# RMS norm of two units at once with its reciprocal root on 128x8, its steps and the weight splits spread over each group, weight sums on VectorE

## The chip, the cores and the metric

The kernel runs on one core of one Trainium2 chip. The core has TensorE (matrix products into PSUM), VectorE, ScalarE and GpSimd (elementwise work; VectorE and ScalarE also read PSUM, GpSimd here works on SBUF alone) and SyncE, called SP in the profile, whose queue issues nearly all DMAs. Each engine runs its own instructions strictly in order and waits on semaphores for the others. The metric is the device time of one execution in microseconds, the median of several runs.

## What is computed

Three stages in a chain: a linear attention with decay over 768 steps for 4 batches and 8 heads, a first expert with a maximum of three products, and a second, gated expert behind an RMS norm. The norm and the second expert are where most of the change lies.

```python
# attention: y = r (state + u k v), state = w state + k v, along 768 steps; x = its output, 3072 tokens x 384
# first expert (d_ff 768)
h = np.maximum(np.maximum(x @ w1, x @ w2), x @ w3)
x = h @ w_out
# second expert (d_ff 1536)
rms = np.sqrt(np.mean(x * x, axis=-1, keepdims=True) + 1e-06)
xn = x / rms * rms_g
g = xn @ w_gate
silu = g * (1.0 / (1.0 + np.exp(-g)))
val = xn @ w_val
out = silu * val @ w_out
```

## The kernel before

**Units and pairs.** Tokens are cut into units of 512 columns; the first 512 are two half units for the first expert. Feature dimensions lie on the partitions, tokens on the free axis. The first expert runs through units 0 to 6 (`UNITS`, the last one is `L` = 6), each with 18 slots `a_l1(u, f, w)` (one 128-row block of one of the three products, nine matmuls) and, from unit 1 on, 6 slots `a_out` (nine matmuls each). Between the slots of one unit the attention steps of the next units are put, and until they are used up also the conversion of the weights (`tick`): loads as 64-bit words, an exponent cast on ScalarE, three bit operations on VectorE, and then a split or, for the second expert's weights, a store to `w2d` and the sums of `w_sums` (four subtractions of 128x128 per block f, stored to `w2t`).

**fp32 by three products.** Each fp32 operand is a high part (a cast to fp32r) and a low part (value minus high part). `mm3` (L72 to L74) issues three matmuls for a product. The cast is always on ScalarE, the subtraction on VectorE or GpSimd.

**Second expert.** It runs over three pairs of 512-token units, p = 0, 1, 2, each in 12 groups f (128 hidden features). Each group forms 2x2 blocks with fewer products: `form_steps` makes three sets of combined activations (one, y, two), `w_sums` made the combined weights. In a group, TensorE runs product A into bank a, ScalarE copies it to bank b (`pb`, L753), TensorE runs E (into `px`, L72 to L74 with `px<-f`) and adds to bank b, ScalarE copies E to `es` (L757) and bank b to c (`pc`), TensorE goes on with a, c, b, ScalarE computes `si`, copies c to d (`pd`), VectorE forms `v` and `si` (L773, L776), ScalarE casts `hb` (L704), VectorE subtracts (L705), and forms the second unit's `v` and `h` (L782, L783). `es` and both `v` share three buffers. The `b_out` products of the group before stand in the same group: block d = 0 after E, d = 1 and 2 at the end. After group 11 the even unit's three blocks are copied out (`ob`, L717), and then the odd unit's 12 `b_out` follow from `h2`, with the forms of the next pair beside them.

**Norm.** `rms_steps(u)` (L536 to L579) is a generator for one unit: squares on ScalarE, two additions on GpSimd, split, two matmuls against ones (every partition then holds the sum), and on 128x512: mean on VectorE, square root on ScalarE, four reciprocals of 128x128, a correction of five operations, three scalings. For units 0 and 1 it is drawn two steps a slot beside the first expert's last unit (from slot 2), then `form_steps(0)`. For the later pairs it is drawn four steps at the end of each group from group 2 on.

**Splits of the second expert's weights.** `ws_split` and `wo_split` make high and low parts of block f. For blocks 0 to 2 it is done in the last unit (GpSimd subtracts), for later ones in pair 0, at the end of each group, behind the norm's steps, on ScalarE and VectorE. `ws_raw` and `wo_raw` load the raw blocks; the split blocks are stored to `w2s` through GpSimd's queue and loaded from there in pairs 1 and 2 (`ws_load`).

The order on each engine is the order in which the program is written.

## Time and profile before

| | us |
|---|---|
| median of 3 runs | 949.53 (947.66 to 950.11) |
| the profiled execution, its own time | 948.55 |
| its span, first to last instruction | 946.8 |
| TensorE busy | 875.8 (92%) |
| VectorE busy | 591.3 (62%) |
| ScalarE busy | 394.5 (42%) |
| GpSimd busy | 242.5 (26%) |
| mean granted TensorE clock | 0.969 of full speed |

The rows further down are of that one execution, and times in them are microseconds from the start of the span. The first expert's last unit starts at 418.36 us and the second expert at about 477 us. A granted clock of 1.00 is 2.4 GHz, 0.50 is 1.2 GHz. In a row of the timeline the bracket at the end tells how long the engine stood idle before the instruction and what released it.

### The profile page before, as it was taken

The numbers are of one execution on the slowest core, as the hardware profiler recorded it, in microseconds if no ns is written. First come the engines' busy times: TensorE is split into PE (matmuls) and PEld (weight loads), VectorE is DVE, ScalarE is ACT, GpSimd is POOL, SyncE is SP. The second block draws the span as 40 slices with busy tenths as digits, with TensorE's granted clock in tenths as the row PEclk, the third lists the DMA queues.
The fourth block names the chain that finished last, engine by engine and source line by source line (L and its number), as shares of the span: only waits on it lengthen the run. The fifth ranks groups of instructions, "written<-read, shape, count | busy, mean of one in ns | idle before, by whom it ended". The sixth has DMA issues, their size and how long they took to land.

```text
span 946.8 us, 11983 instructions
## 1 busy us (share of the span) xinstructions
PE 875.8 (92%) x4340; PEld 731.9 (77%) x4340; DVE 591.3 (62%) x876; ACT 394.5 (42%) x744; POOL 242.5 (26%) x239
## 2 busy tenths in 40 slices
PE   7779799999989989999889887999998999999997
PEld 7678788888878878887667665878787778888875
DVE  6999738787787877736665665672453574433342
ACT  3545333323323423313365644553454444444442
POOL 2675643553554543303421000000101000000000
PEclk8789999999999999999889989999999999999999
DMA  6655434455555555443246451153422033433001
GB/s 211 209 159 165 146 117 114 138 167 176 138 175 164 155 174 160 154 160 144 101 167 216 169 194 56 50 233 145 154 102 100 1 109 157 142 109 137 14 34 37
DMA packets 48994, 128.99 MB, mean 136 GB/s; under 512 B 6176, under 2 KB 22560, under 8 KB 44320
## 3 DMA queue, kind: packets, MB, share of 16 engines
q1 hardware_dynamic: 47200, 113.99, 37.1%
q0 software_dynamic: 1728, 14.16, 3.9%
q8 instruction: 36, 0.59, 0.3%
q14 instruction: 30, 0.25, 0.1%
HBM read 92.34 MB, written 33.82 MB: 133 GB/s over the span
## 4 chain that ended last, share of the span: by engine, by line
PE 62%; DVE 19%; ACT 6%; issue 6%; DMA 2%; POOL 2%; SPq 1%; DVEq 0%; POOLq 0%; ACTq 0%
PE px L73 5%; PE px L74 5%; PE px L72 5%; PE pl L72 4%; PE pl L73 4%; PE pl L74 4%; PE pa L74 3%; PE pa L72 3%; PE pa L73 3%; PE pb L72 3%; PE pb L74 3%; PE pb L73 3%; PE py L349 2%; PE pc L72 2%; PE pc L73 2%
## 5 line engine op out<-in xcount | busy, mean ns | idle before, releaser
L72 PE MATMUL pl<-x,w_a 128*128 128x512 f32 (+1 forms) x378 | 144.1, 381 | 9.9 <-DVE c L429 6.4
L73 PE MATMUL pl<-x,w_a 128*128 128x512 f32 (+1 forms) x378 | 138.7, 367 | 0.3 <-DVE x L365 0.3
L74 PE MATMUL pl<-x,w_a 128*128 128x512 f32 (+1 forms) x378 | 138.2, 366 | 0.3 <-POOL w_a L127 0.3
L773 DVE TENSOR_TENSOR v<-pb,es 128x512 f32<-128x512 f32 x36 | 24.9, 691 | 151.9 <-PE pb L74 143.1
L72 PEld LDWEIGHTS pl<-x,w_a 128*128 128x128 f32 x378 | 73.7, 195 | 20.9 <-DVE c L429 5.7
L72 PE MATMUL px<-hb,wo 128*128 128x512 f32 x216 | 84.5, 391 | 3.6 <-ACT hb L704 3.6
L73 PE MATMUL px<-hb,wo 128*128 128x512 f32 x216 | 84.5, 391 | 0.7 <-DVE hb L705 0.7
L74 PE MATMUL px<-hb,wo 128*128 128x512 f32 x216 | 84.2, 390 | 0.0
L74 PEld LDWEIGHTS pl<-x,w_a 128*128 128x128 f32 x378 | 73.5, 194 | 11.5 <-POOL w_a L127 0.5
L73 PEld LDWEIGHTS pl<-x,w_a 128*128 128x128 f32 x378 | 73.7, 195 | 9.7 <-DVE x L365 0.6
L431 ACT CAST h1h<-c 128x512 fp32r<-128x512 f32 (+1 forms) x42 | 23.5, 559 | 119.3 <-DVE c L429 119.3
L349 PE MATMUL py<-Dg,tm 128*96 128x128 f32 x368 | 57.9, 284 | 10.8 <-DVE Dg L302 9.8
L429 DVE TENSOR_TENSOR c<-pl,c 128x512 f32<-128x512 f32 (+1 forms) x84 | 50.6, 602 | 26.7 <-PE pl L74 19.1
L257 ACT ACTIVATE rh<-raw,csb 96x512 fp32r<-96x512 f32 (+1 forms) x48 | 32.1, 715 | 70.1 <-DVE raw L247 55.2
L72 PE MATMUL pb<-f,ws 128*128 128x512 f32 x108 | 44.6, 413 | 15.5 <-ACT pb L753 15.5
L704 ACT CAST hb<-si 128x512 fp32r<-128x512 f32 x36 | 22.3, 621 | 85.7 <-DVE si L776 85.7
L302 DVE COPY_PREDICATED Dg<-csb,pa 128x512 f32<-128x512 uint32 x48 | 35.0, 730 | 36.6 <-PE pa L74 17.7
L349 PEld LDWEIGHTS py<-Dg,tm 128*96 128x96 f32 x368 | 47.0, 170 | 13.5 <-DVE Dg L302 11.8
L118 DVE SCALAR_TENSOR_TENSOR wf<-wraw,wf 128x384 uint32<-128x384 uint32 x60 | 55.5, 924 | 0.0
L72 PEld LDWEIGHTS px<-hb,wo 128*128 128x128 f32 x216 | 40.6, 188 | 13.1 <-ACT hb L704 4.8
L113 DVE SCALAR_TENSOR_TENSOR wf<-wraw,wf 128x384 uint32<-128x384 uint32 x60 | 49.7, 828 | 0.0
L73 PEld LDWEIGHTS px<-hb,wo 128*128 128x128 f32 x216 | 40.6, 188 | 10.0 <-DVE hb L705 1.6
(172 smaller groups left out, 2143.9 us busy)
## 6 DMA issues: line engine op xcount, KB each, us to landing
ws<-w2s SPq DMA_DIRECT2D x24, 1152.0 KB, 5.2
wraw<-in_w2p SPq DMA_DIRECT2D x36, 384.0 KB, 3.6
w2s<-ws POOLq DMA_DIRECT2D x12, 1152.0 KB, 5.8
raw<-in_rkT SPq DMA_DIRECT2D x24, 384.0 KB, 4.3
tm<-in_rkv SPq DMA_DIRECT2D x24, 384.0 KB, 3.9
tm<-in_rkv SPq DMA_DIRECT2D x24, 288.0 KB, 3.1
wraw<-in_w1p SPq DMA_DIRECT2D x18, 384.0 KB, 3.6
w2d<-wf SPq DMA_DIRECT2D x36, 192.0 KB, 3.8
```

Source lines behind the costliest of these rows:

```text
L72: pe.matmul(o, lh, rh, start=start, stop=False, **kw)
L73: pe.matmul(o, lh, rl, start=False, stop=False, **kw)
L74: pe.matmul(o, ll, rh, start=False, stop=stop, **kw)
L113: dve.scalar_tensor_tensor(out=wu, in0=conv_words(n)[0], scalar=29, in1=wu, op0=ALU.logical_shift_right, op1=ALU.bitwise_or)
L118: dve.scalar_tensor_tensor(out=wu, in0=conv_words(n)[1], scalar=0x80000000, in1=wu, op0=ALU.bitwise_and, op1=ALU.bitwise_or)
L257: act.activation(rh[:, :, j], raw[:, 0], AF.Copy, scale=m01[0:96, j:j + 1])
L302: dve.copy_predicated(out=dg, mask=cmask.unsqueeze(1).to_broadcast([128, 4, 128]), data=pa.rearrange("p q j t -> p (q j) t"))
L349: pe.matmul(py[0:96, pr], tm[:, VO + 144 * pr + 48 * j:VO + 144 * pr + 48 * j + 96], s["Dg"][:, 2 * pr + j], start=(c == 0 and j == 0), st ...
L429: dve.tensor_tensor(out=c1[:, :n], in0=p[:, :n], in1=c1[:, :n], op=ALU.max)
L431: act.copy(hh, c1[:, :n])
L704: act.copy(hh, x)
L773: dve.tensor_tensor(out=v1, in0=Bk, in1=es, op=ALU.add)
```

## The change

- `norm_steps(p)` takes the place of `rms_steps(u)`: it does both units of a pair. The sums still come from two matmuls against ones, but only row 0 is copied out (1x512) and stored to a small DRAM tensor `msd`; it is loaded back as 128x8 for both units, the reciprocal root is made there by a bit estimate and four Newton steps on VectorE (16 operations, no square root on ScalarE), stored to `rsd`, and loaded back spread over all partitions; then the six scalings. `sq` has two buffers for it.
- In the pairs, one step of the norm and one of the splits is drawn at each of four places of a group (`back(0)` to `back(3)`), in place of all at the end; the splits' subtractions in pair 0 go to GpSimd.
- In the last unit of the first expert the norm is drawn from slot 1 on; its activations `h1` lie in what becomes `h2`, and the pool of the second expert is opened ahead of slot 0. The forms of pair 0 come in the order one, two, y, with the last set after slot 18.
- `w_sums` runs on VectorE and one tick later, when the third block of f is stored.
- The output blocks are tiles of their own, 128x512, in two buffers, and each is stored by itself.

```diff
     def w_sums(f, g, v):
         def sub(o, a, b):
-            pool.tensor_tensor(out=o, in0=a, in1=b, op=ALU.subtract)
+            dve.tensor_tensor(out=o, in0=a, in1=b, op=ALU.subtract)
...
-            if q == 0:
-                conv_put.g = w
-            elif q == 1:
-                w_sums(f, conv_put.g, w)
+            if q < 2:
+                conv_put.gv.append(w)
+            else:
+                w_sums(f, *conv_put.gv)
+                conv_put.gv = []
...
+        def norm_steps(p):
+            br = sB["r"]
+            us = (2 * p, 2 * p + 1)
+            x = [x2s.pop(u) for u in us]
+            sq = [br.tile([128, 3, 512], F32, tag="sq", bufs=2, name=f"sq{u}") for u in us]
+            for j in range(2):
+                for k in range(3):
+                    act.activation(sq[j][:, k], x[j][:, k], AF.Square)
+                    if k:
+                        pool.tensor_tensor(out=sq[j][:, 0], in0=sq[j][:, 0], in1=sq[j][:, k], op=ALU.add)
+                    yield
+            for j in range(2):
+                sr = br.tile([128, 2, 512], F32R, tag="sr", name=f"sr{us[j]}")
+                act.copy(sr[:, 0], sq[j][:, 0])
+                yield
+                dve.tensor_tensor(out=sr[:, 1], in0=sq[j][:, 0], in1=r32(sr[:, 0]), op=ALU.subtract)
+                yield
+                ps = psx.tile([128, 512], F32, tag="x", name=f"ss{us[j]}") if p == 0 else PX[3]
+                pe.matmul(ps, ones, sr[:, 0], start=True, stop=False)
+                pe.matmul(ps, ones, sr[:, 1], start=False, stop=True)
+                act.copy(sq[j][0:1, 1], ps[0:1])
+                sync.dma_start(msd[p, j:j + 1], sq[j][0:1, 1])
+                yield
+            m, y, t = (br.tile([128, 8], F32, tag=f"n{n}", name=f"n{n}{p}") for n in range(3))
+            sync.dma_start(m, msd[p].rearrange("j (a b) -> (j a) b", b=8))
+            yield
+            yield
...
+            for _ in range(4):
+                dve.tensor_tensor(out=t, in0=y, in1=m, op=ALU.mult)
+                dve.tensor_tensor(out=t, in0=t, in1=y, op=ALU.mult)
+                dve.scalar_tensor_tensor(out=y, in0=t, scalar=1.5, in1=y, op0=ALU.add, op1=ALU.mult)
+            sync.dma_start(rsd[p].rearrange("j (a b) -> (j a) b", b=8), y)
+            for j in range(2):
+                sync.dma_start(sq[j][:, 2], rsd[p, j].partition_broadcast(128))
             yield
             yield
+            for j in range(2):
+                for k in range(3):
+                    dve.scalar_tensor_tensor(out=x[j][:, k], in0=x[j][:, k], scalar=rg_sb[:, k:k + 1],
+                                             in1=sq[j][:, 2], op0=ALU.mult, op1=ALU.mult)
                     yield
+                xr[us[j]] = x[j]
...
-                    if n >= 2:
-                        next(es, None)
-                        next(es, None)
+                    if n >= 1:
+                        for _ in range(2):
+                            if n >= 18 or form_left[0] > 3:
+                                next(es, None)
...
-                    if d == 0:
-                        b_out.ob = br.tile([128, 3, 512], F32, tag="ob", name=f"ob{u}")
-                    ob = b_out.ob
-                    (dve.tensor_copy if d == 1 else act.copy)(ob[:, d], po[d])
-                    if u == NB - 1:
-                        sync.dma_start(out[u, :, d], ob[:, d])
-                    elif d == 2:
-                        sync.dma_start(out[u], ob)
+                    ob = br.tile([128, 512], F32, tag="ob", bufs=2, name=f"ob{u}_{d}")
+                    (dve.tensor_copy if d == 1 else act.copy)(ob, po[d])
+                    sync.dma_start(out[u, :, d], ob)
...
+                def back(n):
+                    if n < 4 or p:
+                        next(wsp, None)
+                    if f >= 2:
+                        next(bg, None)
```

`back(0)` stands behind the copy `pc`, `back(1)` behind `pd`, `back(2)` behind `hb` and the second `si`, `back(3)` at the end of the group. `wsp` yields the two halves of `ws_split(f + 3)` and then `wo_split(f + 2)`, all in pair 0 alone.

How the order moves, at three places. First ScalarE in pair 0, group 8 (`pb_8` opens the group's copies, `pb_9` the next one's; `gv` and `wof` are raw weights, `ws` and `wo` their high parts). Before:

```order
L753 COPY pb_8_4976<-pa_8_4972 128x512 [waits PE_49]
L757 COPY es_8_4981<-px_4336 128x512 [waits PE_49]
L762 COPY pc_8_4989<-pb_8_4976 128x512 [waits PE_49,Activation_49]
L766 ACTIVATE si_8_0_4997<-pa_8_4972 128x512 [waits PE_49]
L769 COPY pd_8_5003<-pc_8_4989 128x512 [waits DVE_49,PE_49]
L704 CAST hb<-si_8_0_4997 128x512 [waits DVE_49]
L778 ACTIVATE si_8_1_4998<-pc_8_4989 128x512 [waits PE_49]
L562 ACT_TABLE_LOAD [waits DVE_49]
L562 ACTIVATE sq_4875<-sq_4875 128x512 [waits Activation_49]
L508 CAST ws_4328<-gv_4964 128x576 [waits DMAHW2_49,DMAHW1_49,DMASW7_49]
L533 CAST wo_4330<-wof_4970 128x384 [waits DMAHW4_49]
L753 COPY pb_9_5054<-pa_9_5050 128x512 [waits PE_49]
```

After, the same group:

```order
L780 COPY pb_8_5007<-pa_8_5003 128x512 [waits PE_49]
L784 COPY es_8_5012<-px_4344 128x512 [waits PE_49]
L789 COPY pc_8_5020<-pb_8_5007 128x512 [waits PE_49,Activation_49]
L516 CAST ws_4336<-gv_4983 128x576 [waits DMAHW5_49,DMAHW6_49,DMASW7_49,Pool_49]
L794 ACTIVATE si_8_0_5030<-pa_8_5003 128x512 [waits PE_49]
L797 COPY pd_8_5036<-pc_8_5020 128x512 [waits DVE_49,PE_49]
L516 CAST ws_4336<-gv_4983 128x576 [waits DMAHW7_49,Pool_49]
L718 CAST hb<-si_8_0_5030 128x512 [waits DVE_49]
L807 ACTIVATE si_8_1_5031<-pc_8_5020 128x512 [waits PE_49]
L541 CAST wo_4338<-wof_4989 128x384 [waits DMAHW0_49]
L780 COPY pb_9_5079<-pa_9_5075 128x512 [waits PE_49]
```

The casts of the split moved from the end of the group to between the copies (the second `ws` cast of before, a row like the first, is left out), and the root with its table load is gone.

Second VectorE in pair 0 from the end of group 5 to the `v` of group 6 (`x_2` is the first unit of the next pair, `n` the 128x8 tiles, `sq` holds the norm). Before:

```order
L782 TENSOR_TENSOR v_5_4782<-pd_5_4759,es_5_4737 128x512 [waits PE_49]
L783 TENSOR_TENSOR h_4332<-v_5_4782,si_5_1_4754 128x512 [waits DVE_49,Activation_49]
L566 RECIPROCAL sq_4547<-sq_4547 128x128
L568 TENSOR_TENSOR sq_4547<-sq_4547 128x512 [waits DVE_49]
...
L575 SCALAR_TENSOR_TENSOR x_2_4467<-x_2_4467,rg_sb,sq_4547 128x512 [waits DVE_49]
L509 TENSOR_TENSOR ws_4022<-gv_4720,ws_4022 128x576 [waits DMAHW5_49,DMAHW6_49,DMASW4_49,Activation_49]
...
L534 TENSOR_TENSOR wo_4329<-wof_4726,wo_4329 128x384 [waits DMAHW0_49,Activation_49]
L773 TENSOR_TENSOR v_6_4849<-pb_6_4814,es_6_4819 128x512 [waits PE_49,Activation_49]
```

After, from the last of the small operations on:

```order
L580 TENSOR_TENSOR n_4769<-n_4769,n_4768 128x8 [waits DVE_49]
L581 SCALAR_TENSOR_TENSOR n_4768<-n_4769,n_4768 128x8 [waits DVE_49]
L812 TENSOR_TENSOR v_5_4836<-pd_5_4783,es_5_4755 128x512 [waits PE_49]
L813 TENSOR_TENSOR h_4340<-v_5_4836,si_5_1_4778 128x512 [waits DVE_49,Activation_49]
L589 SCALAR_TENSOR_TENSOR x_2_4488<-x_2_4488,rg_sb,sq_4513 128x512 [waits DMAHW7_49]
L589 SCALAR_TENSOR_TENSOR x_2_4488<-x_2_4488,rg_sb,sq_4513 128x512
L802 TENSOR_TENSOR v_6_4891<-pb_6_4849,es_6_4854 128x512 [waits PE_49,Activation_49]
```

The splits' subtractions are gone from here, the small operations stand ahead of the second `v` of group 5, and the first scaling waits for a DMA (the broadcast), with the `v` of group 6 behind it.

Third ScalarE where pair 0's even unit ends (`px` holds the finished blocks, `hb<-h` are the casts for the odd unit). Before:

```order
L769 COPY pd_11_5219<-pc_11_5205 128x512 [waits DVE_49,PE_49]
L704 CAST hb<-si_11_0_5213 128x512 [waits DVE_49]
L778 ACTIVATE si_11_1_5214<-pc_11_5205 128x512 [waits PE_49]
L717 COPY ob_5254<-px_4333 128x512 [waits PE_49]
L717 COPY ob_5254<-px_4335 128x512 [waits PE_49]
L704 CAST hb<-h_4332 128x512 x2
```

After:

```order
L797 COPY pd_11_5234<-pc_11_5220 128x512 [waits DVE_49,PE_49]
L718 CAST hb<-si_11_0_5228 128x512 [waits DVE_49]
L807 ACTIVATE si_11_1_5229<-pc_11_5220 128x512 [waits PE_49]
L729 COPY ob_0_5269<-px_4341 128x512 [waits PE_49]
L729 COPY ob_2_5281<-px_4343 128x512 [waits DMAHW2_49,PE_49,Activation_49]
L718 CAST hb<-h_4340 128x512 x2
```

The rows stand as before, but the second copy now waits for a DMA, the store of the first.

## Rows read from the trace of the kernel before

**Rows 1.** timeline of TensorE (start, duration, line): last unit, first and last E

```profile
418.36 0.39 PE L72 MATMUL pl<-x,w_a 128*128 128x512 f32 x1
...
477.75 0.39 PE L72 MATMUL px<-f,ws 128*128 128x512 f32 x1
...
609.69 0.39 PE L72 MATMUL px<-f,ws 128*128 128x512 f32 x1
...
647.71 0.39 PE L72 MATMUL px<-f,ws 128*128 128x512 f32 x1
...
761.65 0.39 PE L72 MATMUL px<-f,ws 128*128 128x512 f32 x1
...
799.68 0.39 PE L72 MATMUL px<-f,ws 128*128 128x512 f32 x1
...
902.63 0.39 PE L72 MATMUL px<-f,ws 128*128 128x512 f32 x1
```

**Rows 2.** waits; engine and line, whom it waited for: us in total, times, longest

```profile
PE pb L72 <- ACT pb L753: 15.5, 10, 4.3
...
PE py L349 <- DVE Dg L302: 9.8, 7, 3.3
```

**Rows 3.** timeline of ScalarE in pair 0, between two groups

```profile
587.85 1.28 ACT L562 ACT_TABLE_LOAD   x1 [3.58 <-DVE sq L560]
...
589.68 1.23 ACT L508 CAST ws<-gv 128x576 fp32r<-128x576 f32 x2
...
591.22 0.57 ACT L753 COPY pb<-pa 128x512 f32<-128x512 f32 x1
```

**Rows 4.** timeline of TensorE in pair 1, a gap and slow matmuls

```profile
718.77 0.50 PE L72 MATMUL pb<-f,ws 128*128 128x512 f32 x1 [1.97 <-ACT pb L753]
...
720.03 0.60 PE L74 MATMUL pa<-f,ws 128*128 128x512 f32 x1
...
722.99 0.61 PE L72 MATMUL pb<-f,ws 128*128 128x512 f32 x1
```

**Rows 5.** stretches; last three columns: granted clock, DMA share, GB/s

```profile
720.00:724.00 4.00, 4.00 (x12) 3.10 (x11) 0.00 (x0) 1.56 (x3) 0.00 (x0) 0.57 0.00 0
```

**Rows 6.** timeline of VectorE at the start, six small operations in a chain

```profile
2.90 1.37 DVE L204 TENSOR_TENSOR ptab<-ptab 96x4 f32<-96x4 f32 x6
```

**Rows 7.** DMA issues: count, KB each, median us from issue to landing

```profile
x2d<-x2s SPq DMA_DIRECT2D x18, 256.0 KB, 2.1
...
out<-ob SPq DMA_DIRECT2D x3, 256.0 KB, 3.2
...
wsb<-in_wd SPq DMA_DIRECT2D x1, 1.5 KB, 1.6
rg_sb<-in_rg SPq DMA_DIRECT2D x1, 1.5 KB, 8.0
```

**Rows 8.** timeline of VectorE in pair 2, group 11, undisturbed

```profile
908.34 0.69 DVE L773 TENSOR_TENSOR v<-pb,es 128x512 f32<-128x512 f32 x1 [5.26 <-PE pb L74]
909.14 0.69 DVE L776 TENSOR_TENSOR si<-v,si 128x512 f32<-128x512 f32 x1
```

**Rows 9.** groups of instructions by line and shape: count | busy us, mean ns

```profile
L575 DVE SCALAR_TENSOR_TENSOR x<-x,rg_sb,sq 128x512 f32<-128x512 f32 x18 | 12.7, 747 | 0.2
...
L370 DVE TENSOR_TENSOR hl<-py,hl 96x128 fp32r<-96x128 f32 x20 | 5.6, 280 | 9.3 <-ACT x L369 9.3
```

**Rows 10.** timeline of the last unit, GpSimd and VectorE together

```profile
432.80 1.43 POOL L509 TENSOR_TENSOR ws<-gv,ws 128x576 fp32r<-128x576 f32 x1 [2.98 <-ACT ws L508]
...
433.29 1.48 DVE L432 TENSOR_TENSOR h1l<-c,h1h 128x512 fp32r<-128x512 f32 x1
```

**Rows 11.** timeline where pair 0's even unit ends

```profile
619.41 0.59 ACT L717 COPY ob<-px 128x512 f32<-128x512 f32 x1 [1.37 <-PE px L74]
...
620.76 0.58 ACT L717 COPY ob<-px 128x512 f32<-128x512 f32 x1 [0.77 <-PE px L74]
...
621.92 0.49 PE L72 MATMUL px<-hb,wo 128*128 128x512 f32 x1 [1.19 <-ACT hb L704]
```

More of the change, by code (lines that the diff above doesn't have):

```diff
@@ L405, in att_steps @@
                 yield lambda i=i: fin(i)
-    hs = {}
+    hs, sB = {}, {}
     def a_l1(u, f, w):
@@ L553, in rms_steps @@
             yield
-            dve.tensor_tensor(out=sl, in0=sq[:, 0], in1=r32(sh), op=ALU.subtract)
             yield
-            ps = psx.tile([128, 512], F32, tag="x", name=f"ss{u}") if u < 2 else PX[3]
-            pe.matmul(ps, ones, sh, start=True, stop=False)
-            pe.matmul(ps, ones, sl, start=False, stop=True)
-            m, r0, t0 = sq[:, 0], sq[:, 1], sq[:, 2]
-            dve.tensor_scalar(out=m, in0=ps, scalar1=1.0 / DM, scalar2=1e-6, op0=ALU.mult, op1=ALU.add)
-            yield
@@ L562, in rms_steps @@
-            act.activation(t0, m, AF.Sqrt)
-            yield
-            for h in range(4):
-                cs = slice(128 * h, 128 * h + 128)
-                dve.reciprocal(r0[:, cs], t0[:, cs])
-                yield
-            dve.tensor_tensor(out=t0, in0=r0, in1=r0, op=ALU.mult)
-            dve.tensor_tensor(out=t0, in0=t0, in1=m, op=ALU.mult)
-            yield
-            dve.tensor_scalar(out=t0, in0=t0, scalar1=-0.5, scalar2=1.5, op0=ALU.mult, op1=ALU.add)
-            dve.tensor_tensor(out=r0, in0=r0, in1=t0, op=ALU.mult)
@@ L598, in form_steps @@
             yield
-            sets = forms[p] = []
-            for n, x in enumerate((one, y, two)):
+            sets = forms[p] = [None] * 3
+            for n in ((0, 2, 1) if p == 0 else range(3)):
+                x = (one, y, two)[n]
                 if n < 2:
@@ L617, in rwkv_moe_kernel @@
             todo = steps[pos:5 + 5 * UNITS[u + 1][-1]] if u < L else []
+            if u == L:
+                tick(NJ + 1 - tick_n[0])
+                sT.close()
+                sB["r"] = sBr.enter_context(tc.tile_pool(name="b_r", bufs=1, side="right"))
             done = 0
@@ L641, in rwkv_moe_kernel @@
                     if n == 0:
-                        tick(NJ + 1 - tick_n[0])
-                        sT.close()
-                        sB["r"] = sBr.enter_context(tc.tile_pool(name="b_r", bufs=1, side="right"))
-                        x2_load(0)
+                        for v in range(2):
+                            x2_load(v)
                         for f in range(2):
@@ L651, in early @@
                         def early():
-                            for v in range(2):
-                                yield from rms_steps(v)
-                                yield
+                            yield from norm_steps(0)
                             yield from form_steps(0)
@@ L730, in rwkv_moe_kernel, with split_steps @@
             s3, a22, a23 = ((zh[:, k], zl[:, k]) for k in range(3))
-            def rest():
-                for v in range(2 * p + 2, 2 * p + 4):
-                    if v < NB:
-                        yield from rms_steps(v)
-                        yield
-            rs = rest()
+            bg = norm_steps(p + 1) if p + 1 < NB // 2 else iter(())
+            def split_steps(f):
+                if p == 0 and f + 3 < F2:
+                    for hf in range(2):
+                        ws_split(f + 3, hf, pool)
+                        yield
+                    if f + 4 < F2:
+                        ws_raw(f + 4)
+                if p == 0 and f + 2 < F2:
+                    wo_split(f + 2, pool)
+                    if f + 3 < F2:
+                        wo_raw(f + 3)
+                    yield
             pend = None
@@ L762, in rwkv_moe_kernel @@
                 act.copy(C, Bk)
+                back(0)
                 prod(A, a12, G1, False, False)
@@ L769, in rwkv_moe_kernel @@
                 act.copy(Dk, C)
+                back(1)
                 prod(Bk, s4, V1, False, False)
@@ L779, in rwkv_moe_kernel @@
                 low()
+                back(2)
                 prod(Dk, a23, V2, False, True)
@@ L789, in rwkv_moe_kernel @@
                         x2_load(v)
[L790 to L805 removed]
+                back(3)
+                if p and f + 4 < F2:
                     ws_load(f + 4)
[L807 removed]
+            for _ in bg:
                 pass
```

65 lines of the change are left out of this document (22 added, 43 removed).

## The prediction

> **What bounds the kernel now.** I read the time of the E product of each group first, then the waits, then one stall in detail. TensorE sets the end: from the first E product of a pair to its last there are 453 matmuls (one group of 33, ten of 42), and in pair 2, which has no norm and no weight split beside it, they take 902.63 - 799.68 = 102.95 us, 0.2273 us each [rows 1]. The same 453 take 131.94 us in pair 0 and 113.94 us in pair 1 [rows 1], so these two hold 29.0 and 11.0 us too much. From the first matmul of the last unit of the first expert to the first E product there are 24 slots of 9, four matmuls of the norm and three of product A, 223 in all: 50.7 us at that rate, against 477.75 - 418.36 = 59.39 us [rows 1], 8.7 us too much. So 48.7 us are at stake, and all lie where the norm and the splits run.
>
> The reader sees in the waits that TensorE mostly waits for ScalarE's copy of bank a into pb [rows 2]. One stall shows how: ScalarE stood 3.58 us at the norm's square root until VectorE had the mean, loaded a table (1.28 us), then had the splits' casts before it, and so copied pb only at 591.22 [rows 3]. ScalarE runs in order: whatever waits there holds the copies of the banks. A stall can cost more than itself. After a gap of 1.97 us, eight matmuls from 720.03 to 722.99 ran at 0.6 us [rows 4], and the granted clock of those four microseconds was 0.57, a mixture of the 1.2 and the 2.4 GHz level [rows 5]. At the lower level a matmul lasts 0.2 us longer, so such a spell is 1.6 us.
>
> **The norm of a pair at once.** The square root, its table loads, the reciprocals of 128x512 and their corrections go. Their place is taken by a row copy, four DMA hops in series (mean to DRAM, back as 128x8, result to DRAM, broadcast back) and 16 VectorE operations on 128x8. Six operations about that small took 1.37 us [rows 6], 0.23 each, so 16 take 3.2 to 3.7 us. A small hop I take at 2.0 us, near the 1.6 us of a lone 1.5 KB load; the broadcast writes 256 KB, as much as the stores that took 2.1 and 3.2 us [rows 7].
>
> In the pairs the norm starts in group 2 and advances four steps a group; the mean leaves at the end of group 4. It is back in SBUF some 5 us into group 5, while VectorE gets to the small operations about 9 us into it (its v starts 5.7 and its si 6.5 us after E in an undisturbed group [rows 8], hb behind them), so nobody waits there. Two things then run late. The second v of group 5 is held 3.2 us; the copy es of group 6 needs its buffer and so holds ScalarE, which costs TensorE about 0.9 us. And the first two scalings by the norm (0.75 us each [rows 9]) stand ahead of the v of group 6 on VectorE and wait for the broadcast: the result is sent 12.5 us into group 5 and lands at 14.6, the broadcast at 17 to 18, so v starts at 18 to 19 instead of 15.9. Behind it wait the hb cast and the next pb copy, which has about 2 us to spare. Both together: 1.5 us a pair, 0.5 to 5 by the hops. The norm's four matmuls (0.9 us) stay.
>
> In the last unit the steps go two a slot from slot 1. Both units' squares lie together and come early, and I expect about 1 us of waiting at each of the two sums. But VectorE then stands some 4 us at the scalings until the broadcast lands, with the maxima of later slots behind; four banks cover 8 us of this, and what is left, with the form operations that follow, costs about 2.5 us. Left over: 4.5 us of the 8.7 (2 to 8), **gain 4.2 us**. The forms' new order (the one that needs the second x buffer last, the others before) lets pair 0 start without waiting for them; that is part of pair 0's gain.
>
> **Splits on GpSimd, spread over the group.** 28 subtractions leave VectorE in pair 0, and their casts no longer stand in one block before pb. ScalarE's work in groups 2 and 3 stays near full: seven operations of about 0.6, the split's three (1.23 for the two wide ones [rows 3]) and three or four squares, 8 to 8.5 of 9.5 us. I price that at 0.5 us, the one table load that remains (group 0) at 0.7, the norm's lateness at 1.5 and its matmuls at 0.9: 3.6 us left of pair 0's 29.0 (1.5 to 9), **gain 25.4 us**. Pair 1 has the norm alone: 2.4 us left of 11.0 (1 to 6), **gain 8.6 us**.
>
> A VectorE operation on SBUF that begins while GpSimd subtracts ends half a microsecond after it: 1.48 us beside a subtraction of 1.43 us [rows 10], against 0.69 for si alone [rows 8]. Such a hit on si delays the hb cast by 0.3 to 1.4 us; in the new order the second subtraction overlaps si by about 0.4 us, less than ScalarE's slack.
>
> The Trainium skill speaks against this move: "SBUF — State Buffer", section "Who interferes with whom", has a tensor_tensor with both inputs in SBUF contend with GpSimd's reads for one exclusive pair of ports, the loser blocked for the whole instruction. The trace agrees, 1.48 against 0.69 us; taken for every group it makes the rival "port" below the forecast, by the overlap it is 0.3 us inside the slack.
>
> **Weight sums on VectorE.** 48 subtractions of 128x128 leave GpSimd for VectorE, 0.28 us each by the nearest shape, 96x128 [rows 9]: 13.4 us over units 2 to 5, where VectorE has idle time and GpSimd now holds it up less. The sums come one tick later, when the stores to w2d no longer read the operands, so nobody waits for those. Behind the four operations two stores stand on SP, and the next exponent cast on ScalarE needs their buffer two slots later, about when they land. I take 0, between -5 (half of TensorE's 9.8 us of waiting for Dg [rows 2]) and +5.
>
> **Output tiles.** The three blocks of a unit now share two buffers, so the copy of d = 2 waits until the store of d = 0 has landed; the built order has that wait at all six unit ends. At the end of an even unit ScalarE copies d = 0 from 619.41 (0.59 us, so until 620.00) and d = 2 from 620.76; behind them is the hb cast for which TensorE waits until 621.92 [rows 11]. The store can leave at 620.05 and lands 2.1 to 3.2 us later [rows 7], so d = 2 starts 1.4 to 2.5 us late, and the gap of 1.19 us becomes 2.6 to 3.7. I count one spell of low clock for a gap of that size, 1.6 us. Three even ends: 3 x (1.95 + 1.6) = 10.6 us. At the two odd ends inside, the next pair's pb stands behind: 1.85 us each, 3.7, without a spell. At the very end the last store leaves about 1 us later. **Loss 15.3 us** (7 with the shortest landings and full clock, 22 with the longest and a spell each time).
>
> **Sum.** The profiled execution took 948.55 us (span 946.8). 948.55 - 4.2 - 25.4 - 8.6 + 0 + 15.3 = 925.65; its own time is 0.98 us below the median of 949.53, so 926.6 us.
>
> **Rivals.**
> - *Port.* If in each of ten groups the hb chain is held by a whole subtraction (1.43 us [rows 10]) without slack, pair 0 keeps 14 us instead of 3.6: 937. For: ScalarE's slack is thin in groups 2 and 3. Against: v reads PSUM, and the subtractions fall mostly beside it or beside nothing.
> - *Slower.* The hops queue behind other traffic: a 1.5 KB load took 8.0 us when loads stood ahead [rows 7]. Two hops lie behind the small operations in each of three chains, with VectorE, and soon ScalarE and TensorE, standing: at 8.0 us, 6 x 6 = 36 us more, 962. It decides from about 3.8 us more a hop (6 x 3.8 = 22.9). Against: SP issues nothing else between these hops.
> - *Better.* Unit ends at 7 instead of 15.3 us and units 2 to 5 rid of 5 us of stalls: 913.
> - *No change.* The stalls were ScalarE's amount of work, not its order; then they come back elsewhere: 949. Against: its work in a group stays below 9.5 us.
>
> **How the numbers follow.** Forecast 0.59 (915 to 938), port 0.13, better 0.12, no change 0.08, slower 0.08. A change of 0.3%, 2.8 us, is about what a measurement of this kernel can tell. Faster takes the forecast, port and better: 0.84; same 0.08; slower 0.08. The range, 908 to 944, holds those three and leaves out the last two.
>
> **What would show it.** Right: first to last E product near 107 us in pair 0 and 105 in pair 1; no square root on ScalarE; the first v of group 6 two to three microseconds late, behind a scaling that waits for a DMA; at the unit ends a copy of ob on ScalarE that waits for a store, a TensorE gap of about 3 us behind it and a low clock after. Wrong: pair 0 above 115 us, VectorE standing over 5 us at the scalings, or unit ends with a gap of 1.2 us as before.

## The result and the profile after

The changed kernel takes 921.38 us (median of 4 runs, 919.71 to 921.64), against 948.6 us for the kernel before on the same chip (4 runs). The ratio is 0.9711 (95% interval 0.9687 to 0.9736). The forecast was 926.6 us, within 908 to 944. The profiled execution took 919.71 us:

```profile
span 918.0 us, 12000 instructions
## 1 busy us (share of the span) xinstructions
PE 864.8 (94%) x4340; PEld 727.8 (79%) x4340; DVE 565.4 (62%) x890; ACT 384.9 (42%) x735; POOL 252.6 (28%) x219
```

The timeline of TensorE after has the rows that answer to [rows 1] (first matmul of the last unit, then first and last E product of each pair):

```profile
409.90 0.39 PE L74 MATMUL pl<-x,w_a 128*128 128x512 f32 x1
...
468.80 0.40 PE L74 MATMUL px<-f,ws 128*128 128x512 f32 x1
...
577.00 0.39 PE L74 MATMUL px<-f,ws 128*128 128x512 f32 x1
...
616.46 0.39 PE L74 MATMUL px<-f,ws 128*128 128x512 f32 x1
...
723.97 0.39 PE L74 MATMUL px<-f,ws 128*128 128x512 f32 x1
...
765.01 0.39 PE L74 MATMUL px<-f,ws 128*128 128x512 f32 x1
...
869.18 0.39 PE L74 MATMUL px<-f,ws 128*128 128x512 f32 x1
```

Pair 0 takes 108.20 us (before 131.94), pair 1 107.51 (before 113.94), pair 2 104.17 (before 102.95), the last unit 58.90 (before 59.39). The rest of the gain lies where none was forecast: from the first matmul of unit 2 to that of unit 6 it is 270.92 us, and it was 279.89.

The waits of TensorE (engine, line, whom it waited for: us in total, times, longest) have new heads; the copies to pb [rows 2] are down to two, 1.22 and 1.20 us at the two odd unit ends:

```profile
PE pl L74 <- DVE c L437: 10.6, 5, 4.4
PE px L74 <- ACT hb L718: 9.7, 5, 2.6
...
PE pb L74 <- ACT pb L780: 2.4, 2, 1.2
```

**Pairs.** VectorE's timeline from group 5 of pair 0 (its E product is at 517.73), with ScalarE's copy es of group 6 ahead:

```profile
528.25 0.59 ACT L784 COPY es<-px 128x512 f32<-128x512 f32 x1
...
530.42 0.68 DVE L812 TENSOR_TENSOR v<-pd,es 128x512 f32<-128x512 f32 x1
...
535.26 1.41 DVE L589 SCALAR_TENSOR_TENSOR x<-x,rg_sb,sq 128x512 f32<-128x512 f32 x2 [2.37 <-DMA sq<-rsd]
536.59 0.68 DVE L802 TENSOR_TENSOR v<-pb,es 128x512 f32<-128x512 f32 x1
```

The scalings wait for the broadcast, and the v of group 6 stands behind them: it starts 18.86 us after that E product, where 18 to 19 was forecast. The interval between E products at this place, group 7, is 11.54 us in place of 9.52 (pair 1: 11.29). The copy es of group 6 is not held: it starts at 528.25, 2.2 us ahead of the second v of group 5, and group 6 takes 9.52 us in both pairs. A second stall was not foreseen. ScalarE's timeline in group 4:

```profile
517.10 0.58 ACT L565 COPY sq<-px 1x512 f32<-1x512 f32 x1 [1.02 <-PE px L564]
517.79 0.57 ACT L780 COPY pb<-pa 128x512 f32<-128x512 f32 x1
```

The norm's row copy waits for the second sum's matmuls, and those for a subtraction on VectorE; the copy to pb stands behind. Group 4 takes 11.95 us, 1.5 more than its 42 matmuls and the norm's four; in pair 1 10.88.

**Last unit.** VectorE, GpSimd and TensorE in their timelines, merged by time:

```profile
439.90 1.42 DVE L589 SCALAR_TENSOR_TENSOR x<-x,rg_sb,sq 128x512 f32<-128x512 f32 x2 [4.82 <-DMA sq<-rsd]
...
441.97 0.50 PE L74 MATMUL pl<-x,w_a 128*128 128x512 f32 x1 [1.70 <-DVE c L437]
...
444.98 2.26 POOL L542 TENSOR_TENSOR wo<-wof,wo 128x384 fp32r<-128x384 f32 x1 [10.73 <-ACT wo L541]
...
445.68 0.69 DVE L606 TENSOR_TENSOR y<-x 128x512 f32<-128x512 f32 x1
446.40 1.39 DVE L607 TENSOR_TENSOR y<-y,x 128x512 f32<-128x512 f32 x1
...
447.21 3.40 POOL L600 TENSOR_TENSOR f<-x,f 128x512 fp32r<-128x512 f32 x2
...
447.83 1.66 DVE L609 TENSOR_TENSOR y<-x,y 128x512 f32<-128x512 f32 x1
449.41 1.74 DVE L610 TENSOR_TENSOR x<-x,x 128x512 f32<-128x512 f32 x1
451.08 1.47 DVE L437 TENSOR_TENSOR c<-pl,c 128x512 f32<-128x512 f32 x2
...
451.81 0.50 PE L74 MATMUL pl<-x,w_a 128*128 128x512 f32 x1 [3.43 <-DVE c L437]
```

VectorE stands 4.82 us at the broadcast, then has six scalings with two maxima between them, then three form operations that last 1.39 to 1.74 us beside GpSimd's subtractions. The form operation ahead of them, at 445.68, keeps its 0.69 us although GpSimd subtracts then too; there it is GpSimd's subtraction that takes longer, 2.26 us against 1.02 for one of the same shape at 433.24. TensorE waits 1.70 us (441.97) and 3.43 us (451.81) for the maxima at L437, and eight matmuls from 452.84 to 455.76 run slowly (about 0.6 us each and not 0.4).

**Unit ends.** Rows that answer to [rows 11], in the timelines of ScalarE and TensorE:

```profile
586.72 0.59 ACT L729 COPY ob<-px 128x512 f32<-128x512 f32 x1 [1.37 <-PE px L76]
589.47 0.59 ACT L729 COPY ob<-px 128x512 f32<-128x512 f32 x1 [2.17 <-DMA out<-ob]
...
590.62 0.50 PE L74 MATMUL px<-hb,wo 128*128 128x512 f32 x1 [2.58 <-ACT hb L718]
```

All three even ends have a gap of 2.57 or 2.58 us (before 1.19), both odd ends one of 1.2 us (before none), and the last matmul is followed by 8.6 us instead of 6.7. In the table of stretches (last three columns: granted clock, DMA share, GB/s) the clock falls after the second even end:

```profile
737.00:743.00 6.00, 5.18 (x15) 3.85 (x16) 4.44 (x8) 2.20 (x5) 0.00 (x0) 0.72 0.89 315
```

It fell after the third as well (0.62 from 882 to 886 us), not after the first (1.00 from 588 to 594).

### The profile page after: what moved, and what is told of

It reads as the page before. It is cut to its first block, busy times and chain, and to the rows that moved or that the text cites. A ratio compares the mean times of both kernels' runs of the same rounds, so it can differ in the third digit from the quotient of the medians.

```text
span 918.0 us, 12000 instructions
## 1 busy us (share of the span) xinstructions
PE 864.8 (94%) x4340; PEld 727.8 (79%) x4340; DVE 565.4 (62%) x890; ACT 384.9 (42%) x735; POOL 252.6 (28%) x219
## 4 chain that ended last, share of the span: by engine, by line
PE 79%; DVE 11%; DMA 3%; issue 3%; ACT 2%; POOL 0%; SPq 0%; DVEq 0%; ACTq 0%
PE pl L74 7%; PE pl L75 7%; PE pl L76 7%; PE px L75 6%; PE px L76 6%; PE px L74 6%; PE py L353 3%; PE pa L74 3%; PE pa L76 3%; PE pa L75 3%; PE po L74 3%; PE po L76 3%; PE po L75 3%; PE pb L74 3%; PE pb L76 2%
## 5 line engine op out<-in xcount | busy, mean ns | idle before, releaser
L74 PE MATMUL px<-hb,wo 128*128 128x512 f32 x216 | 85.9, 398 | 9.7 <-ACT hb L718 9.7
L75 PE MATMUL px<-hb,wo 128*128 128x512 f32 x216 | 86.0, 398 | 1.0 <-DVE hb L719 0.9
L76 PE MATMUL px<-hb,wo 128*128 128x512 f32 x216 | 85.1, 394 | 0.0
L76 PEld LDWEIGHTS pl<-x,w_a 128*128 128x128 f32 x378 | 73.6, 195 | 11.5 <-POOL w_a L129 0.5
L286 POOL TENSOR_SCALAR_AFFINE_SELECT Dg<-a 128x1024 f32<-128x1024 f32 x24 | 27.4, 1140 | 133.1 <-DVE a L283 103.3
L437 DVE TENSOR_TENSOR c<-pl,c 128x512 f32<-128x512 f32 (+1 forms) x84 | 50.8, 605 | 20.1 <-PE pl L76 19.3
L439 ACT CAST h1h<-c 128x512 fp32r<-128x512 f32 (+1 forms) x36 | 19.8, 549 | 98.1 <-DVE c L437 98.1
L74 PEld LDWEIGHTS px<-hb,wo 128*128 128x128 f32 x216 | 41.1, 190 | 20.4 <-ACT hb L718 11.8
L120 DVE SCALAR_TENSOR_TENSOR wf<-wraw,wf 128x384 uint32<-128x384 uint32 x60 | 53.9, 899 | 0.0
L75 PEld LDWEIGHTS px<-hb,wo 128*128 128x128 f32 x216 | 41.3, 191 | 11.5 <-DVE hb L719 3.0
L115 DVE SCALAR_TENSOR_TENSOR wf<-wraw,wf 128x384 uint32<-128x384 uint32 x60 | 48.1, 801 | 0.0
L76 PEld LDWEIGHTS px<-hb,wo 128*128 128x128 f32 x216 | 41.3, 191 | 8.4
```

The costliest lines, as they stand in the source:

```text
L74: pe.matmul(o, lh, rh, start=start, stop=False, **kw)
L75: pe.matmul(o, lh, rl, start=False, stop=False, **kw)
L76: pe.matmul(o, ll, rh, start=False, stop=stop, **kw)
L115: dve.scalar_tensor_tensor(out=wu, in0=conv_words(n)[0], scalar=29, in1=wu, op0=ALU.logical_shift_right, op1=ALU.bitwise_or)
L120: dve.scalar_tensor_tensor(out=wu, in0=conv_words(n)[1], scalar=0x80000000, in1=wu, op0=ALU.bitwise_and, op1=ALU.bitwise_or)
L286: pool.affine_select(out=Dg, in_=a8.unsqueeze(2).to_broadcast([128, H, 128]), pattern=[[0, H], [1, 128]], channel_multiplier=-1, base=0, c ...
```

## The experiments

All but one are the changed kernel with the edits shown; `sums_only` is the kernel before with the edit of the weight sums. For a pair the last column has first to last E product. The ratio is to the kernel before on the same chip; the changed kernel has 0.9711.

| run | median us | ratio (95%) | where |
|---|---|---|---|
| sums_back | 930.63 | 0.9793 (0.9771 to 0.9815) | unit 2 to 6: 279.84 |
| sums_only | 940.84 | 0.9906 (0.9874 to 0.9938) | unit 2 to 6: 270.92 |
| sums_late_pool | 923.23 | 0.9715 (0.9697 to 0.9732) | unit 2 to 6: 270.92 |
| ob3 | 909.19 | 0.9572 (0.9556 to 0.9589) | pair 2: 102.95 |
| split_dve | 928.33 | 0.9775 (0.9758 to 0.9792) | pair 0: 114.15 |
| split_block | 926.69 | 0.9763 (0.9746 to 0.9780) | pair 0: 113.46 |
| scal_pair | 917.26 | 0.9651 (0.9632 to 0.9669) | pairs 106.17, 105.70 |
| hop_twice | 931.67 | 0.9804 (0.9780 to 0.9828) | pairs 112.14, 111.06 |
| scal_unit | 919.09 | 0.9679 (0.9658 to 0.9700) | last unit: 56.32 |
| form_dve | 920.13 | 0.9693 (0.9673 to 0.9713) | last unit: 58.11 |
| best | 903.11 | 0.9523 (0.9504 to 0.9543) | pair 0: 109.27 |
| best2 | 899.62 | 0.9480 (0.9464 to 0.9496) | pair 0: 105.35 |

The last column is read from one execution of each run, and such a reading scatters: group 7 took 11.54 to 13.43 us in pair 0 and 10.83 to 13.44 in pair 1 in the six traces (the changed kernel, `sums_back`, `sums_late_pool`, `ob3`, `scal_unit`, `form_dve`) in which no edit touches it. The longest of each held a spell of low clock.

### The weight sums: place or engine

`sums_back` takes both back, `sums_only` adds both to the kernel before, `sums_late_pool` keeps the new place on the old engine.

```diff
-            dve.tensor_tensor(out=o, in0=a, in1=b, op=ALU.subtract)
+            pool.tensor_tensor(out=o, in0=a, in1=b, op=ALU.subtract)
...
-            if q < 2:
-                conv_put.gv.append(w)
-            else:
-                w_sums(f, *conv_put.gv)
-                conv_put.gv = []
+            if q == 0:
+                conv_put.g = w
+            elif q == 1:
+                w_sums(f, conv_put.g, w)
```

> The changed kernel with the weight sums alone put back: on GpSimd and in the tick of the second third. Theory A, the sums held GpSimd in front of the diagonal blocks Dg: the stretch from the first matmul of unit 2 to that of unit 6, 270.9 us in the changed kernel, goes back to about 279.9 us, the waits for Dg return to TensorE, and the time is 921.4 + 9.0 = 930.4 us (928 to 932). Theory B, something else in the change made that stretch shorter: 921.4 us (920 to 923), stretch 271 us.

> The kernel before with the weight sums alone changed: on VectorE and one tick later. Theory A: units 2 to 5 lose their waits, 948.6 - 9.0 = 939.6 us (937 to 941), the later pairs stay as they were. Theory B: 948.6 us (947 to 950). If sums_back shows the 9 us and this run does not, the gain needs the rest of the change as well.

> The changed kernel with the weight sums back on GpSimd, but at their new place, one tick later. sums_back and sums_only showed that the sums make 9.2 us. Theory A, GpSimd stood waiting at them (for the words that VectorE had not finished, for the store that read the operand), and one tick later nothing is waited for: 921 to 923 us, the stretch from unit 2 to unit 6 at 271 to 273 us. Theory B, it is their work, or the way they share SBUF with VectorE, that holds the diagonal blocks, wherever they stand: 927 to 931 us, stretch 277 to 280 us.

Theory A held in the first two to a tenth of a microsecond in the stretch: the sums make some 9 us, with or without the rest of the change. The timelines of `sums_back` show how, GpSimd, VectorE and TensorE merged by time:

```profile
327.06 1.31 POOL L136 TENSOR_TENSOR wf<-wf 128x128 f32<-128x128 f32 x1 [2.84 <-DVE wf L120]
331.14 0.46 POOL L136 TENSOR_TENSOR wf<-wf,wf 128x128 f32<-128x128 f32 x1 [2.77 <-DMA w2d<-wf]
...
332.63 1.09 POOL L285 TENSOR_SCALAR_AFFINE_SELECT Dg<-a 128x1024 f32<-128x1024 f32 x1
...
333.75 0.74 DVE L305 COPY_PREDICATED Dg<-csb,pa 128x512 f32<-128x512 uint32 x1 [3.85 <-POOL Dg L285]
...
339.90 0.68 PE L352 MATMUL py<-Dg,tm 128*96 128x128 f32 x4 [1.46 <-DVE Dg L305]
```

GpSimd waits at a sum for VectorE's words, then for the store that reads the operand. Behind it stands the diagonal block Dg; VectorE waits 3.85 us for that, comes late to the next one too, and TensorE waits for it, 1.46 us at 339.90. In the waits of `sums_back` GpSimd stood 55.9 us at the sums (22.4 for the words, 17.4 for the store, 16.1 put down to issue). The third run decides between place and engine: on GpSimd, one tick later, the stretch is 270.92 us too. It is the tick; the engine adds nothing that these runs can tell. (Its time, 923.23 us, is 0.2 above theory A's range. 1.9 us by medians remain to the changed kernel, 0.4 by ratios; the intervals overlap.)

### A third output buffer

```diff
-                    ob = br.tile([128, 512], F32, tag="ob", bufs=2, name=f"ob{u}_{d}")
+                    if d == 2:
+                        ob = r32(br.tile([128, 2, 512], F32R, tag="sr", name=f"ob{u}_{d}")[:, 0])
+                    else:
+                        ob = br.tile([128, 512], F32, tag="ob", bufs=2, name=f"ob{u}_{d}")
```

> The changed kernel with a third buffer for the output blocks: the block d = 2 is copied into the first half of the norm's tile sr, which is idle at the unit ends. Theory A, the copy's wait for the store of d = 0 is what the unit ends lose: the even ends' gap goes from 2.58 to 1.2 us, the odd ends' gap of 1.2 us goes, the end after the last matmul from 8.6 to about 6.7 us: 3 x 1.4 + 2 x 1.2 + 1.9 = 8.5 us, and up to 3 us more for the two spells of low clock: 910 to 913 us. Theory B, ScalarE is late there by its own amount of work and the wait is cover for it: within 2 us of 921.4 us.

Theory A at each place; the time, 909.19 us, is 0.8 under its range. The same place in `ob3`, ScalarE and TensorE:

```profile
586.83 0.58 ACT L732 COPY ob<-px 128x512 f32<-128x512 f32 x1 [1.37 <-PE px L76]
588.19 0.58 ACT L732 COPY ob<-px 128x512 f32<-128x512 f32 x1 [0.77 <-PE px L76]
...
589.35 0.50 PE L74 MATMUL px<-hb,wo 128*128 128x512 f32 x1 [1.19 <-ACT hb L718]
```

The waits for the store are gone, gaps are 1.19 us at the even and none at the odd ends, no spell of low clock follows any of them, and 6.8 us stand behind the last matmul. Two buffers cost 12.2 us by the medians, 11.4 by the spans.

### Pair 0: the splits' engine and their place

`split_dve` leaves the splits spread over the group, with VectorE subtracting; `split_block` also puts them back in one block at the group's end.

```diff
-                        ws_split(f + 3, hf, pool)
+                        ws_split(f + 3, hf, dve)
...
-                    wo_split(f + 2, pool)
+                    wo_split(f + 2, dve)
...
-                    if n < 4 or p:
-                        next(wsp, None)
...
                 back(3)
+                for _ in wsp:
+                    pass
```

The last two pieces are in `split_block` alone.

> The changed kernel with the subtractions of pair 0's splits on VectorE as before, but still spread over the group. Theory A, what pair 0 gained came from spreading the casts on ScalarE, and VectorE has room for the subtractions: 920 to 924 us, first to last E product of pair 0 within 2 us of 108.2 us. Theory B (the port): GpSimd's subtractions hold VectorE and cost pair 0 time, so it becomes faster without them: 916 to 919 us, pair 0 at 103 to 106 us. Theory C: VectorE's order is as tight as ScalarE's was, a subtraction that waits for its cast holds v and si: 926 to 935 us, pair 0 at 113 to 122 us.

> The changed kernel with the splits of pair 0 as in the kernel before: on VectorE and in one block at the end of each group; the norm and all else stay new. It divides the 23.7 us that pair 0 gained. split_dve gave 114.2 us from the first to the last E product of pair 0, against 108.2 us. Theory A, the place of the casts (a block ahead of the copy pb) made most of the loss: 122 to 128 us, and 936 to 942 us in all. Theory B, the old norm (square root, table loads, reciprocals) made most of it: 113 to 117 us, and 927 to 931 us.

`split_dve` met theory C at its lower edge, 928.33 us and pair 0 at 114.15 us; theory B (GpSimd's subtractions cost pair 0 time) is refuted, since taking them away costs 6 us (2.2 of it in group 7, with a spell of low clock). In `split_block` theory B held for pair 0, 113.46 us; the time, 926.69 us, is 0.3 under its range. So of pair 0's 23.7 us, 18.5 came without any move of the splits. Of these, 6.3 lie in group 0, which took 14.18 us before and 7.87 in `split_block`. TensorE of the kernel before stood there for a form:

```profile
480.80 0.55 PE L73 MATMUL px<-f,ws 128*128 128x512 f32 x1 [2.66 <-DVE f L587]
```

The granted clock from 480 to 488 us was 0.57. The new order of the forms takes this wait away; no run changes that order alone. The other 12.2 us lie in groups 1 to 10, where the norm stands. No run tells how much of them comes from the root, its table loads and the reciprocals that are gone, and how much from spreading the norm's steps.

The waits from 468 to 582 us in `split_dve` and from 468 to 578 us in the changed kernel tell why the engine matters (engine, line, whom it waited for: total us, times, longest). First `split_dve`:

```profile
DVE ws L517 <- ACT ws L516: 25.8, 15, 5.8
...
DVE v L802 <- PE pb L76: 7.1, 2, 5.3
```

Then the changed kernel:

```profile
DVE v L802 <- PE pb L76: 44.3, 9, 8.3
POOL ws L517 <- ACT ws L516: 30.7, 17, 5.8
```

With the subtractions on VectorE, v no longer waits for TensorE: it stands behind a subtraction that waits for ScalarE's cast. On GpSimd that wait holds nobody. Spreading the splits on VectorE gained nothing (114.15 against 113.46 us, each with one spell of seven slow matmuls in group 7); the block on GpSimd was not run, so whether spreading helps there is open.

### The broadcast on the path

`scal_pair` and `scal_unit` draw empty steps ahead of the scalings (three in the pairs, five in the last unit), `hop_twice` adds a hop.

```diff
             yield
             yield
+            for _ in range(0 if p == 0 else 3):
+                yield
             for j in range(2):
                 for k in range(3):
                     dve.scalar_tensor_tensor(out=x[j][:, k], in0=x[j][:, k], scalar=rg_sb[:, k:k + 1],
```

In `scal_unit` the range is `5 if p == 0 else 0`. In `hop_twice`:

```diff
+            sync.dma_start(rs2[p], rsd[p])
             for j in range(2):
-                sync.dma_start(sq[j][:, 2], rsd[p, j].partition_broadcast(128))
+                sync.dma_start(sq[j][:, 2], rs2[p, j].partition_broadcast(128))
```

> The changed kernel with three more steps between the broadcast and the scalings in pairs 0 and 1 alone. Theory A, the stall of group 7 (11.54 and 11.29 us in place of 9.52) is the v of group 6 behind two scalings that wait for the broadcast: both fall to 9.5 to 9.7 us, 3.7 us in all, and the time to 917 to 918.5 us. Theory B, the v of a later group is then the late one: within 1 us of 921.4 us.

> The changed kernel with one more hop in the norm's chain: the result is copied from DRAM to DRAM before it is broadcast, which should take some 2 us. Theory A, the broadcast stands on the path in all three chains, because VectorE waits at the scalings with v or the maxima behind it: every microsecond of the hop is paid three times, 6 us and up to two spells of low clock more: 926 to 931 us. Theory B, four banks and ScalarE's slack take it up: 921 to 923 us.

> The changed kernel with five more steps between the broadcast and the scalings in the last unit alone, so that VectorE meets the scalings some 2.5 slots later. Theory A, the two gaps of 1.70 and 3.43 us and the spell of low clock behind them come from VectorE standing 4.8 us at the broadcast: the stretch from the first matmul of unit 6 to the first E product, 58.9 us, falls to 52 to 56 us and the time to 915 to 918.5 us. Theory B, they come from the amount of work (six scalings, four form operations of 1.4 to 1.7 us beside GpSimd) in too few slots, and only move: 920 to 924 us.

Theory A in the pairs: with the scalings later, group 7 takes 9.52 us in both, and no other interval grows. The other way round, `hop_twice` took 931.67 us, 0.7 above theory A's range. SyncE and VectorE at that place show the added hop, 1.86 us from its issue to the broadcast's:

```profile
534.48 0.50 SPq L584 DMA_DIRECT2D rs<-rsd  x1
536.34 0.80 SPq L586 DMA_DIRECT2D sq<-rs  x2
...
540.66 1.42 DVE L591 SCALAR_TENSOR_TENSOR x<-x,rg_sb,sq 128x512 f32<-128x512 f32 x2 [5.29 <-DMA sq<-rs]
```

Group 7 grew by 3.97 and 3.62 us, the last unit by 2.72: 10.3 us for three hops of 1.9 (5.7 us). The rest is low clock and a later broadcast: in both pairs seven slow matmuls followed the longer gap (0.2 us each), in the last unit twelve and not eight, and in pair 0 the scalings started 4.3 us after the issue of the broadcast, not 3.3. By the ratios the difference is 8.8 us.

In `scal_unit` both theories hold in part, and its interval overlaps that of the changed kernel. The first gap goes and the unit takes 56.32 us instead of 58.90, 0.3 above theory A's range, but one gap of 2.96 us with slow matmuls stays. VectorE and GpSimd ahead of it:

```profile
451.31 3.48 DVE L612 TENSOR_TENSOR x<-x,x 128x512 f32<-128x512 f32 x1
...
451.73 2.50 POOL L602 TENSOR_TENSOR f<-x,f 128x512 fp32r<-128x512 f32 x2
```

A subtraction of 0.68 us ended only 0.56 us after the last of GpSimd's. That leads to the next run.

### The first form's subtractions on VectorE

```diff
-                    split(h[:, k], lo[:, k], x[:, k], pool if p == 0 and n == 0 else dve)
+                    split(h[:, k], lo[:, k], x[:, k], dve)
```

> The changed kernel with the three subtractions of the first form of pair 0 on VectorE in place of GpSimd; nothing else moves. In the last unit VectorE's form operations last 1.4 to 1.7 us beside GpSimd's and the gap of 3.43 us follows. Theory A (the port): VectorE is held until GpSimd's subtraction ends, so three subtractions of 0.69 us of its own are cheaper than that: the gap falls under 2 us, the stretch from the first matmul of unit 6 to the first E product from 58.9 to 55.5 to 57.5 us, the time to 918 to 920.5 us. Theory B (the amount): VectorE gets 2 us more to do in the slots that are late already: the gap grows to 4 to 5.5 us, the stretch to 59.5 to 61 us, the time to 922 to 924 us.

Inconclusive by time (its interval overlaps that of the changed kernel), in the trace, of the longest of its four executions, on A's side but short of it: the gap falls from 3.43 to 2.44 us, the unit from 58.90 to 58.11. Taking the subtractions from GpSimd gains about 1 us here, not 2.

### Together

`best` has `ob3`, both later scalings, `form_dve` and one more step ahead of the second sum; `best2` also drops one of the two steps behind the 128x8 load in the pairs (the second piece below).

```diff
                 dve.tensor_tensor(out=sr[:, 1], in0=sq[j][:, 0], in1=r32(sr[:, 0]), op=ALU.subtract)
                 yield
+                if p and j:
+                    yield
...
             yield
-            yield
+            if not p:
+                yield
             dve.tensor_scalar(out=m, in0=m, scalar1=1.0 / DM, scalar2=1e-6, op0=ALU.mult, op1=ALU.add)
```

> The changed kernel with what the runs so far point to: a third output buffer (12.2 us by ob3), the scalings three steps later in the pairs (4.1 us by scal_pair) and five in the last unit (2.3 us by scal_unit), the second sum of the norm one step later in the pairs (1.5 and 0.5 us of stall in group 4), and the first form's subtractions on VectorE (2 us if VectorE was held by GpSimd). If these add up: 921.4 - 12.2 - 4.1 - 2.3 - 1.5 - 2 = 899 us (897 to 902). If the gains overlap or a wait takes the place of one that is gone: 903 to 908 us.

> The run named best with one wait step less in the pairs' norm, so that the small operations and the sending of the result stand where scal_pair has them, while the second sum stays a step later. In best, the interval of group 7 in pair 0 is 13.40 us (gap 1.97 us and a spell of low clock), because ScalarE's split cast waited 2.99 us for a weight load that SyncE issued only behind the sending of the result and the broadcast. Theory A, the order on SyncE is the cause: group 7 goes to 9.5 us, pair 0 from first to last E product from 109.3 to 105.3 us, the time from 903.1 to 899 us (898 to 900.5). Theory B, ScalarE or VectorE is full there: group 7 stays over 11 us and the time at 902 to 904 us.

`best` met its second case, 903.11 us. Group 4 fell to 10.77 us, but two of the norm's matmuls had moved on to group 5 (10.01 us, 9.65 before), so the two groups gained 0.8 us together and not 1.5. Group 7 of pair 0 took 13.40. SyncE and ScalarE there:

```profile
526.59 0.32 SPq L584 DMA_DIRECT2D rsd<-n  x1
528.00 0.80 SPq L586 DMA_DIRECT2D sq<-rsd  x2
528.88 0.38 SPq L508 DMA_DIRECT2D gv<-w2d  x1
...
536.55 0.67 ACT L516 CAST ws<-gv 128x576 fp32r<-128x576 f32 x1 [2.99 <-DMA gv<-w2d]
```

The extra step had moved the 16 small operations behind the last product of their group, so the result left 5.4 us after the E product of group 6 (521.17) and not 3.1 us after it, as in the changed kernel (530.53, E at 527.38). The weight loads stand behind it on SyncE's queue, and the one that ScalarE's cast needs in group 7 came late: issued 7.7 us after the E product of group 6 and not 5.4, it took 7.2 us to land and not 5.4. With the operations back in their place in `best2`, group 7 is at 9.52 us, pair 0 at 105.35, and the time 899.62 us: theory A. In the last unit the two edits are worth more together than apart: it takes 53.96 us, 4.9 less than in the changed kernel, where `scal_unit` gained 2.6 and `form_dve` 0.8. This kernel beats both, by 5.2% the one before (5.0 to 5.4%), with TensorE busy for 96% of its span:

```profile
span 897.6 us, 11995 instructions
## 1 busy us (share of the span) xinstructions
PE 857.4 (96%) x4340; PEld 724.5 (81%) x4340; DVE 561.5 (63%) x893; ACT 384.9 (43%) x735; POOL 245.5 (27%) x216
```

## Why the prediction was right, and where it was not

The sign and the range held; by spans the change is 28.8 us (946.8 to 918.0), the sum had 22.9. Its terms:

| term | predicted | measured in the trace |
|---|---|---|
| last unit | -4.2 | -0.5 |
| pair 0 | -25.4 | -23.7 |
| pair 1, without the odd end's gap | -8.6 | -7.7 |
| weight sums | 0 (-5 to +5) | -9.0 |
| output tiles | +15.3 (7 to 22) | +11.5 |

With 0.5 us at the start these make -28.9. It came this near partly by luck, since errors offset: three terms were 6.3 us too hopeful, two 12.8 us too dear.

- **Weight sums, wrong term.** The sum took 0 and half of the waits for Dg [rows 2] as its bound. The prediction said itself that one tick later nobody would wait for the stores, and then gave that no price: GpSimd's wait goes with all that stood behind it. TensorE's waits in this stretch were 4.2 us for Dg and 2.2 for a late h1l, and none over 0.15 us is left; matmul by matmul, some 8 of the 9.0 us arise at these waits. The move to VectorE, which the prediction costed, did nothing. Nor was it right that nobody waits: VectorE waits 10.8 us at the sums for w2d stores, in 4 places; TensorE has no wait in the stretch all the same.
- **Last unit, wrong size.** That VectorE would stand some 4 us at the scalings was right (4.82). "Four banks cover 8 us of this" was the step that failed: the 16 small operations stand ahead of the wait and two scalings behind it, so VectorE takes no maximum from 430.80 to 441.23, 10.4 us; then the other scalings and the forms come, and the maxima are late a second time. Little was lost at the two sums (0.2 us), where 2 us were expected. Left are 8.2 us of the 8.7, not 4.5.
- **Pair 0, right in amount and in the late v, wrong in two terms and in what it credits.** 5.25 us are left: 0.65 in group 0, 0.9 for the norm's matmuls, 1.5 for the second sum ahead of pb (not foreseen), 2.0 at group 7, the rest 0.2. Of the 1.5 us forecast for the norm's lateness, the 0.9 for a held copy es did not come (es waited for no buffer, group 6 took 9.52 us); the late v alone cost the 2.0. Nor did the 0.5 us for a full ScalarE in groups 2 and 3 (9.52 and 9.54 us). The prediction gave the credit to the casts out of the block and to VectorE's relief alike; the runs give 18.5 us to what is left when the splits stay, the new norm with its spread steps and the freed order of the forms, some 5 to 6 to the subtractions' engine, and nothing to spreading the splits on VectorE.
- **Pair 1.** 3.3 us are left instead of 2.4, at the same two places. There are no splits here, so the 7.7 us gained are the norm's; no run divides them between its new operations and the spreading of its steps.
- **Output tiles, right mechanism, too dear.** A store landed 2.1 us after its issue, the short end of [rows 7]; 2.65 was taken. So 1.39 us for each even end, not 1.95; two spells of about 1.5 us in this execution, not three (six of the other eight traces with two buffers have three); 1.2 for each odd end, not 1.85; at the end 1.9, not 1. Sum 4.2 + 3.0 + 2.4 + 1.9 = 11.5 us.
- **Rivals.** "Port" is refuted for the pairs (`split_dve`, and 5.25 us left where it had 14), and costs about 1 us in the last unit, where the overlap is with form operations. The Trainium skill, "SBUF — State Buffer", section "Who interferes with whom", says of such pairs: "Issue order, not op shape, decides who blocks." The 3.48 us above agree that one is held to about the other's end. On which one, the starts in the traces don't settle it: VectorE's operation at 527.05 began after GpSimd's at 526.99 and was held, as the page has it, but the one of 3.48 us began first, at 451.31 against 451.73, and was held too. And pair 0 shows that this prices nothing by itself: what matters is whether the held operation is on the path. "Slower" did not come, with hops of 1.4 and 1.6 us for 4 KB (2.0 was taken), though 3.9 us for the broadcast, and 4.3 for the 4 KB load in pair 1, where nobody waited for it; but `hop_twice` puts its turning point nearer than the prediction did: 1.9 us more in each chain cost 10.3 us, so by an estimate in proportion the forecast's 22.9 us would be gone at some 4.2 us a chain (22.9 x 1.9 / 10.3), 2.1 us a hop in place of 3.8. "Better" named the right places, the unit ends and units 2 to 5; the last unit took 3.7 us of it back and the pairs 2.6. "No change" is refuted.

## What to carry to other kernels

Before costing a moved operation by its duration, ask what it waits for where it stood and what is queued behind it: here the same four subtractions a block, on the same engine, were worth 9 us in all one tick later. A chain through DRAM is cheap only if no in-order queue (VectorE's, ScalarE's, or SyncE's with the loads behind) reaches its consumer before it lands, so place the consumer by the landing and the loads ahead of the sends. When a buffer count falls below the pieces of one burst, price it by the landing of the first store.

## What was not expected of the hardware

- A broadcast of a row to 128 partitions, 256 KB, took 3.9 us from issue to landing (median of the changed kernel, 3.3 to 4.7), an output store of as many bytes 2.0 (2.0 to 3.1).
- VectorE operations of 0.17 us on 128x8 are held by GpSimd too: one of them lasted 0.97 us beside a subtraction of 1.01, in `best` one lasted 1.41 beside one of 1.44.
- A gap of 1.2 us of TensorE at a unit end was never followed by a low granted clock in these traces; one of 2.6 us was in 24 of 27 places: after the first even end of the changed kernel no matmul was slow, in `scal_pair` thirteen were (granted clock 0.50 from 588 to 594 us), with the same gap. So the same wait there cost between 1.4 and about 4 us.
